# One SBUF port in the order planner, the first loads and clears in another order, and the last two steps of a weight's conversion on VectorE unless late

## The chip, the cores and the metric

The kernel runs on one core of a Trainium2 chip. The metric is the device time of one execution in microseconds (us); of the kernel before, three timed runs are given. The profiled execution is one more run, and its span (first to last instruction) lies inside its own time.

## The reference

Causal attention with a cumulative bias, and two matrix-product blocks behind it. All is float32, and the weights arrive as float64 words that the kernel converts itself.

```
scores = q @ k.T / sqrt(64)                      # 4 batches, 8 heads, 576 tokens, 64 wide
cum    = cumsum(max(s, 0))
scores = where(causal, -1e9, scores + min(-(cum[:, None] - cum[None, :]), 0))
x      = softmax(scores) @ v                     # -> [2304, 512]
x      = (s2 * relu(x @ w_in)**2 + b) @ w_out    # 512 -> 2048 -> 512
out    = max(x @ w1, x @ w2, x @ w3) @ w_fin     # 512 -> 3 x 768 -> 512
```

## The kernel before

A float32 product is made of three passes of a split pair: each operand has a part `hi` and a rest `lo` in the matmul type, and `mm3` (L224) multiplies hi by hi, hi by lo and lo by hi. So every operand has a `lo` step, a subtraction (`minus`, L221/222), behind its `hi` step.

The work stands in four stages. **Attention** goes in jobs of two heads: the first four jobs do the first 320 queries of a batch (part A), the next four the other 256 (part B), the other twelve a whole batch's pair of heads (part W). In a job `turn` transposes q and k (L430), `qk` makes scores (L447) and adds the bias with a one-hot row times the table `dd` (L449), `least` (L461) takes the row minimum on VectorE, `expo` (L467) is on ScalarE, `turn_p` transposes the probabilities (L508), `av` multiplies by v (L527), and `x_copy` (L532) leaves the result. **The first block, part a** uses half of the 2048 columns (`wa_in`, `wa_out`), and its matmuls fill whatever TensorE leaves free beside attention. **Part b** uses the other half (`wb_in`, `wb_out`, converted beside attention and parked in DRAM) in eight halves of a batch. **The second block** (`wt`, `wfin`) ends the run.

A weight piece is converted in nine steps (`weight_steps`, L240): a load, an ACT step (`wsa`/`stage`/`wg`, L255), four VectorE steps (L258, L260, L264, L266), the `hi` copy (L215 on ACT), and the two last ones, step 7 (L222: the rest of `hi`) and step 8 (L270: the sum that is `lo`). 16 pieces of 128x512 belong to part a, 32 of 128x256 to part b, 24 of 128x384 to `wt`, and 6 of 128x512 to `wfin`.

The order on every engine is fixed ahead of the run by `Plan.order` (L81): a list of steps with a cost on one or several engines, a priority and needs. It takes at each point the engine with the earliest start, and there the step of best priority. Where a step names two engines, the first is the rule, and the second is taken when it would be done earlier by more than LATE (L52). So the engine named first matters, and in `convert` (L687) the last two steps name GpSimd (Pool) first:

```
shift, either = dve_fast(n) - 0.06, {"Pool": pool_(n), "DVE": dve(n)}
```

Before the plan's steps come the clears and the bias table in written order (L306 to L358): `s` is loaded four times on 32 partitions each, VectorE sums it up (L316) and makes five differences `df` (L321), ScalarE rounds and VectorE splits them into `dd` (L324). GpSimd clears `qn`, `kn`, `vn` (L342) and the tails of the probability tiles `pp` (L351). SP issues the loads of q, k, v and weights in its own order.

Of the kernel before, what the change touches and what calls it, by code (L numbers as in the profile page):

```python
# [8 lines left out]
F32 = mybir.dt.float32  # L9
# [9 lines left out]
P = 128  # L19
# [4 lines left out]
ST2 = 3  # L24
COLD = 15

# [32 lines left out]
class Plan:  # L59
# [21 lines left out]
    def order(self):  # L81
        n = len(self.steps)
# [57 lines left out]
        for done in range(n):  # L140
# [34 lines left out]
def fused_kernel(ctx, tc, q, k, v, s, w_in, w_out, ms, mb, w1, w2, w3, w_fin, out,  # L175
# [142 lines left out]
    df = atp.tile([P, OFF[-1] + W[-1]], F32, name="df", tag="p2")  # L318
    for i in range(NC):
        mid = QS[i] + QN[i] // 2  # L320
        nc.vector.tensor_scalar(df[:, OFF[i]:OFF[i] + W[i]], cum[:, :W[i]], -1.0, cum[:, mid:mid + 1], op0=ALU.mult, op1=ALU.add)  # L321
    for a, b in ((0, OFF[3]), (OFF[3], OFF[4]), (OFF[4], OFF[4] + W[4])):
        nc.scalar.activation(dh[:, :b - a].bitcast(F32R), df[:, a:b], AF.Copy)
        nc.vector.scalar_tensor_tensor(dd[:, a:b], dh[:, :b - a], lower, df[:, a:b], op0=ALU.mult, op1=ALU.add)  # L324


# [11 lines left out]

    qn, kn = (atp.tile([P, NC, 2, D], F32, name=x) for x in ("qn", "kn"))
    vn = [atp.tile([P, NC, 2, D], F32, name=f"vn{i}") for i in range(2)]  # L340
# [8 lines left out]
    for j in range(2):  # L349
        for i in range(NC):  # L350
            nc.gpsimd.memset(pp[j][i][:, W[i]:], 0.0)  # L351
        nc.gpsimd.memset(pp[j][0][LAST:, :], 0.0)

# [240 lines left out]
    add(("begin",), {"SP": 1.05}, 0, -1e9, [], lambda: None)  # L594
    add(("s_b",), "SP", (2, 2), 30.0, [], load_sb)
    jobs = [Job(n, n % NP, "AB"[n // NP]) if n < 2 * NP else Job(n, n - NP, "W") for n in range((B + 1) * NP)]
    t0 = 0.0
    for job in jobs:
# [26 lines left out]
        for x, u in enumerate(units):  # L625
# [3 lines left out]
            ready = [("oh", n)] + [("copy", z, n, y) for z in "qk" for y in range(2)]  # L629
            add(("qk", n, u), "PE", 5 * (k1 - k0) / 2400 + 0.25, at[u], ready + [("after", z) for z in same] + order, qk, job, u,  # L630
                take=[("sm", [("least", n, u, j)]) for j in range(2)], **a)
# [14 lines left out]
        for x, u in enumerate(units):  # L646
            i, k0, k1, c0, c1 = UNITS[u]
            for j in range(2):
# [3 lines left out]
                m = (c1 - c0) * QN[i]  # L652
                add(("turn_p", n, u, j), "PE", 0.109 * (c1 - c0), t, [("exp", n, i, j)] + order, turn_p, job, u, j, take=[("sm", [("copy_p", n, u, j)])], **a)
                over, take = [("after", ("copy_p", n, units[0], j))], []
# [32 lines left out]
    def convert(name, z, piece, stage_tile, prios, needs, ring_st, ring_a, **k):  # L687
# [3 lines left out]
        def step(on=None):  # L691
# [390 lines left out]
```

## Time and profile before

| what | us |
| --- | --- |
| median of three runs (range) | 1014.78 (1014.14 to 1016.34) |
| the profiled execution, its own time | 1016.21 |
| its span | 1014.4 |
| TensorE (PE) busy in the span | 965.1 |
| VectorE (DVE) busy | 496.7 |
| ScalarE (ACT) busy | 451.2 |
| GpSimd (POOL) busy | 307.4 |

TensorE is busy for 95% of the span. Its busy time counts pipelined matmuls with modelled ends, so a busy stretch need not be one at peak, and the granted clock says whether it ran at 2.4 or 1.2 GHz. What any change can take away is the time in which TensorE is idle or at the lower clock.

### The profile page before, as it was taken

Reading aid. Unit: us, or ns where it says so; the run is one execution under the profiler, and the core shown is the slowest. Engines: PE = TensorE matmul, PEld = TensorE weight load, DVE = VectorE, ACT = ScalarE, POOL = GpSimd, SP = SyncE. Lnnn points to the kernel's source line nnn. Section 1 sums busy time; section 2 is a strip of 40 time slices with the busy share of each in tenths; the row PEclk is TensorE's granted clock in tenths of the full one; section 3 lists DMA queues with packets and bytes.
Section 4 is the critical chain, followed back from the end, with each engine's and each line's share of the span. In section 5 each row is a group of like instructions: output and inputs, shape, how many; then the busy total and the mean of one; then the engine's idle time right before and its main releaser. Section 6 shows DMA issues by size and latency. Waiting matters only on the chain.

```text
span 1014.4 us, 17966 instructions
## 1 busy us (share of the span) xinstructions
PE 965.1 (95%) x6532; PEld 877.1 (86%) x6532; DVE 496.7 (49%) x1205; ACT 451.2 (44%) x1210; POOL 307.4 (30%) x398
## 2 busy tenths in 40 slices
PE   3878899999999999999989899999999999999998
PEld 2656788878789779999979899999999999999997
DVE  5888677776752341222799943323942222222221
ACT  4866787877865573332444443334321212121111
POOL 4564444554422103222576732222510000000000
PEclk9889899999999999999989899999999999999999
DMA  6554256556630300381255451313201010100000
GB/s 169 149 159 120 63 169 188 152 162 177 175 85 23 86 17 26 132 306 54 81 156 162 126 170 54 88 38 106 90 16 47 16 47 17 48 16 32 1 32 32
DMA packets 120633, 96.12 MB, mean 95 GB/s; under 512 B 70240, under 2 KB 104032, under 8 KB 120544
## 3 DMA queue, kind: packets, MB, share of 16 engines
q1 hardware_dynamic: 120448, 94.82, 32.0%
q8 instruction: 52, 0.85, 0.4%
q14 instruction: 37, 0.30, 0.1%
q10 hardware_dynamic: 96, 0.15, 0.0%
HBM read 67.67 MB, written 27.26 MB: 94 GB/s over the span
## 4 chain that ended last, share of the span: by engine, by line
PE 78%; DVE 9%; DMA 4%; issue 4%; POOL 3%; ACT 2%; SPq 0%; POOLq 0%; DVEq 0%; ACTq 0%
PE mm L226 20%; PE mm L227 20%; PE mm L228 20%; PE ps L447 5%; PE pt L508 5%; PE px L527 4%; PE pr L430 2%; PE ps L449 1%; POOL gbl L222 1%; DMA qn<-in_q_dram 1%; DMA xs<-x_d 1%; DVE g L849 1%; DVE wsa L258 1%; PE pr L498 1%; DVE wsa L260 1%
## 5 line engine op out<-in xcount | busy, mean ns | idle before, releaser
L226 PE MATMUL mm<-yh,wt 128*128 128x384 f32 x432 | 146.2, 339 | 0.0
L228 PE MATMUL mm<-yh,wt 128*128 128x384 f32 x432 | 146.2, 338 | 0.0
L227 PE MATMUL mm<-yl,wt 128*128 128x384 f32 x432 | 146.2, 338 | 0.0
L999 DVE TENSOR_TENSOR u<-mm,u 128x384 f32<-128x384 f32 x72 | 40.1, 556 | 186.5 <-PE mm L228 186.4
L853 ACT ACTIVATE g<-g 128x256 f32<-128x256 f32 (+1 forms) x128 | 56.5, 442 | 127.3 <-DVE g L849 127.0
L849 DVE TENSOR_SCALAR g<-mm 128x256 f32<-128x256 f32 (+1 forms) x128 | 58.3, 456 | 96.3 <-PE mm L228 82.0
L467 ACT ACTIVATE pp<-pp,mn 64x64 f32<-64x64 f32 (+4 forms) x160 | 88.4, 555 | 27.4 <-DVE mn L461 27.2
L227 PE MATMUL mm<-gbl,wb_out 128*128 128x320 f32 (+2 forms) x256 | 79.4, 310 | 10.3 <-POOL gbl L222 10.2
L508 PE MATMUL pt<-ident,pp 128*128 128x128 f32 x480 | 80.6, 287 | 6.3 <-DVE mn L461 3.0
L222 POOL TENSOR_TENSOR ga<-g,ga 128x320 fp32r<-128x320 f32 (+1 forms) x60 | 49.0, 817 | 120.3 <-ACT ga L215 106.8
L226 PE MATMUL mm<-xhi,wa_in 128*128 128x320 f32 (+1 forms) x256 | 83.4, 326 | 0.0
L222 POOL TENSOR_TENSOR gbl<-g,gbh 128x256 fp32r<-128x256 f32 (+1 forms) x61 | 52.5, 861 | 100.3 <-ACT gbh L215 100.2
L447 PE MATMUL ps<-k,q 64*128 64x288 f32 (+4 forms) x384 | 75.4, 455 | 7.5 <-DVE mn L461 5.8
L226 PEld LDWEIGHTS mm<-yh,wt 128*128 128x128 f32 x432 | 81.1, 188 | 1.3
L227 PEld LDWEIGHTS mm<-yl,wt 128*128 128x128 f32 x432 | 81.1, 188 | 1.3
L226 PE MATMUL mm<-ga,wa_out 128*128 128x320 f32 (+2 forms) x256 | 82.0, 320 | 0.0
L228 PEld LDWEIGHTS mm<-yh,wt 128*128 128x128 f32 x432 | 81.1, 188 | 0.0
L461 DVE CUSTOM_DVE_ANT_0 pp<-late_keys,ps 64x64 f32<-64x64 f32 (+4 forms) x160 | 61.7, 421 | 38.1 <-PE ps L449 37.9
L215 ACT ACTIVATE pt<-pt 128x256 f32<-128x256 f32 (+3 forms) x184 | 73.4, 432 | 15.3 <-PE pt L508 14.1
L226 PE MATMUL mm<-gbh,wb_out 128*128 128x320 f32 (+2 forms) x256 | 78.0, 305 | 0.8 <-ACT gbh L215 0.6
L227 PE MATMUL mm<-xlo,wa_in 128*128 128x320 f32 (+1 forms) x256 | 76.9, 300 | 0.8 <-POOL xlo L222 0.8
L228 PE MATMUL mm<-gbh,wb_out 128*128 128x320 f32 (+2 forms) x256 | 77.5, 303 | 0.0
(176 smaller groups left out, 2453.6 us busy)
## 6 DMA issues: line engine op xcount, KB each, us to landing
wst<-in_moe_w_dram SPq DMA_DIRECT2D x24, 384.0 KB, 3.4
wb_d<-wbs SPq DMA_DIRECT2D x21, 256.0 KB, 2.9
out_dram<-o SPq DMA_DIRECT2D x18, 256.0 KB, 2.1
kn<-in_k_dram SPq DMA_DIRECT2D x32, 128.0 KB, 3.0
vn<-in_v_dram SPq DMA_DIRECT2D x32, 128.0 KB, 2.7
wst<-in_moe_w_out_dram SPq DMA_DIRECT2D x8, 512.0 KB, 3.9
wb_in<-wb_d SPq DMA_DIRECT2D x8, 512.0 KB, 7.6
wb_out<-wb_d SPq DMA_DIRECT2D x8, 512.0 KB, 9.1
```

The costliest lines, as they stand in the source:

```text
L215: nc.scalar.activation(dst, src, AF.Copy, scale=1.0 if scale is None else scale)
L222: ENGINES[on].tensor_tensor(dst, a, b, op=ALU.subtract)
L226: nc.tensor.matmul(ps, lhs[0], rhs[0], start=first, stop=False)
L227: nc.tensor.matmul(ps, lhs[0], rhs[1], start=False, stop=False)
L228: nc.tensor.matmul(ps, lhs[1], rhs[0], start=False, stop=last)
L447: nc.tensor.matmul(ps[:, :k1 - k0], qt[job.n][r, QS[i]:QS[i] + P], kt[job.n][r, k0:k1], start=True, stop=False)
L461: nc.vector.tensor_tensor_reduce(out=pp[j][i][:n, k0:k1], in0=late_keys[:n, a:a + k1 - k0], in1=ps_.pop((job.n, u, j))[:n, :k1 - k0], scal ...
L467: nc.scalar.activation(p[:n, :w], p[:n, :w], AF.Exp, bias=mns[job.n, j][:n, i:i + 1], scale=-1.0, accum_out=sums[job.n % 2][:n, j, i:i + 1])
L508: nc.tensor.transpose(pt[:, c - c0, :], pp[j][i][:, c * P:(c + 1) * P], ident)
L527: nc.tensor.matmul(px_[job.n][hf][j * D:(j + 1) * D, a0 - h0:h1 - h0], vn[job.n % 2][:, c, j, :], columns(job, pr["p", job.n, j], c, c + 1 ...
L849: nc.vector.tensor_scalar(st["g", f], st["u", f][:, :n], 0.0, None, op0=ALU.max)
L853: nc.scalar.activation(st["g", f], st["g", f], AF.Square)
```

## The change

The planner gets a table of steps that it counts as users of one SBUF port of VectorE and GpSimd together: every GpSimd step, and on VectorE every weight step and the named ones in PORT. Such a step starts in the plan no earlier than the other engine's last such step ends, less 0.1 us. Nothing in the hardware is switched; only the planned order moves. COLD, the time in which the plan doubles TensorE's costs, goes from 15 to 8.

The last two steps of a weight's conversion name VectorE first, and GpSimd only when late. The four loads of `s` go to ScalarE's queue, so SP starts with q and k. `qn` and `kn` are cleared on VectorE and `vn` on GpSimd, and only the partitions of the short chunks. The bias differences 3 and 4, and the tails of `pp` 3 and 4, become planned steps behind a "pre" step for each engine's opening. 26 transposes of the identity open TensorE's row.

```diff
-COLD = 15
+COLD = 8
+WARM = 26
...
+    PORT = ("square", "lo", "hi", "x_hi", "x_lo", "xb_lo", "lo_h", "lo_y")
+    OVERLAP = 0.1
...
+        port = {"Pool": 0.0, "DVE": 0.0}
+
+        def has_port(i, e):
+            key = self.steps[i][0]
+            return e == "Pool" or e == "DVE" and (key[0] == "w" or key[0] in self.PORT or key[0][:-1] in self.PORT)
...
+            if has_port(i, e):
+                t = max(t, port["DVE" if e == "Pool" else "Pool"] - self.OVERLAP)
...
     for g in range(4):
-        (nc.sync if g < 2 else nc.scalar).dma_start(s0[g * NH:(g + 1) * NH], s.rearrange("b h s -> (b h) s"))
+        nc.scalar.dma_start(s0[g * NH:(g + 1) * NH], s.rearrange("b h s -> (b h) s"))
+    SHORT = (SPLIT // P, NC - 1)
+    for t in (qn, kn):
+        for c in SHORT:
+            nc.vector.memset(t[LAST:, c], 0.0)
...
-    for t in (qn, kn, *vn):
-        nc.gpsimd.memset(t[D:, :, :, :], 0.0)
+    for t in vn:
+        for c in SHORT:
+            nc.gpsimd.memset(t[LAST:, c], 0.0)
...
+    def warm():
+        ps = bank("warm")
+        for _ in range(WARM):
+            nc.tensor.transpose(ps[:, :P], ident, ident)
...
+    for e, cost in (("DVE", 8.2), ("ACT", 7.3), ("Pool", 5.0)):
+        add(("pre", e), e, cost, -1e9, [], lambda: None)
+    add(("warm",), "PE", 0.213 * WARM / 2, -1e9, [], warm, take=[("sm", [("warm",)])])
+    for i in range(3, NC):
+        add(("dd", i), "DVE", 2.2, 1.0 + i, [("pre", "DVE")], rest_d, i, att=True)
+    add(("pp",), "Pool", 1.2, 4.0, [("pre", "Pool")], rest_p, att=True)
...
+        either2 = {"DVE": dve(n), "Pool": pool_(n)}
...
-                 ("DVE", shift, (4,), []), ("DVE", dve(n), (5,), []), (either, 0, (6,), []), (either, 0, (7,), []))
+                 ("DVE", shift, (4,), []), ("DVE", dve(n), (5,), []), (either2, 0, (6,), []), (either2, 0, (7,), []))
```

What the order becomes is seen best in three places. The first is SP's row of DMA issues from the start, before (`qn`, `kn`, `vn` are q, k and v tiles, 128x2x64 full chunks and 64x2x64 the short one; `wg` and `stage` hold a 512 KB weight piece):

```order
L309 DMA s_123<-in_s_dram 32x576 x2
L406 DMA qn<-in_q_dram 64x2x64
L406 DMA kn<-in_k_dram 64x2x64
L251 DMA wg<-in_moe_w_in_dram 128x512
L406 DMA vn_159<-in_v_dram 64x2x64
L251 DMA wg<-in_moe_w_in_dram 128x512
L406 DMA vn_160<-in_v_dram 64x2x64
L251 DMA wg<-in_moe_w_in_dram 128x512
L404 DMA qn<-in_q_dram 128x2x64 x2
L404 DMA kn<-in_k_dram 128x2x64 x2
```

The same row with the change:

```order
L429 DMA qn<-in_q_dram 128x2x64 x2
L431 DMA qn<-in_q_dram 64x2x64
L429 DMA kn<-in_k_dram 128x2x64 x2
L431 DMA kn<-in_k_dram 64x2x64
L266 DMA wg<-in_moe_w_in_dram 128x512
L429 DMA vn_130<-in_v_dram 128x2x64 x2
L431 DMA vn_130<-in_v_dram 64x2x64
L266 DMA wg<-in_moe_w_in_dram 128x512
L429 DMA vn_131<-in_v_dram 128x2x64 x2
L431 DMA vn_131<-in_v_dram 64x2x64
L266 DMA wg<-in_moe_w_in_dram 128x512
L266 DMA stage<-in_moe_w_in_dram 128x512 x2
```

The full chunks of the first q and k moved ahead of all weights; five weight pieces, where there were three, now stand ahead of the second job's q, which follows this piece of the row.

The second place is GpSimd's row in the second half of part b, before (`gbl` is the `lo` of an activation that TensorE's next product waits for, `wsa` and `wt` are steps 7 and 8 of a weight piece):

```order
L222 TENSOR_TENSOR wsa<-wsa,wt_6105 128x384
L222 TENSOR_TENSOR gbl_6113<-g,gbh_6112 128x256
L222 TENSOR_TENSOR gbl_6113<-one 128x2
L222 TENSOR_TENSOR gbl_6115<-g,gbh_6114 128x256
L222 TENSOR_TENSOR gbl_6115<-one 128x2
L270 TENSOR_TENSOR wt_6105<-wsa,wst 128x384
L222 TENSOR_TENSOR gbl_6117<-g,gbh_6116 128x256
L222 TENSOR_TENSOR gbl_6117<-one 128x2
L222 TENSOR_TENSOR wsa<-wsa,wt_6105 128x384
```

And with the change:

```order
L237 TENSOR_TENSOR gbl_6142<-g,gbh_6141 128x256
L237 TENSOR_TENSOR gbl_6142<-one 128x2
L237 TENSOR_TENSOR gbl_6144<-g,gbh_6143 128x256
L237 TENSOR_TENSOR gbl_6144<-one 128x2
L237 TENSOR_TENSOR gbl_6146<-g,gbh_6145 128x256
L237 TENSOR_TENSOR gbl_6146<-one 128x2
```

The weight steps have left GpSimd's row; in all of part b it holds nothing but `gbl`.

The third is VectorE's row in the same half, before (`g` is the relu that leaves PSUM):

```order
L258 TENSOR_SCALAR wsa<-wsa 128x384
L849 TENSOR_SCALAR g<-mm 128x256
L260 SCALAR_TENSOR_TENSOR wsa<-wst,wsa 128x384
L849 TENSOR_SCALAR g<-mm 128x256
L264 TENSOR_SCALAR wst<-wsa 128x384
L266 SCALAR_TENSOR_TENSOR wst<-wst 128x384
L258 TENSOR_SCALAR wsa<-wsa 128x384
L849 TENSOR_SCALAR g<-mm 128x256
L260 SCALAR_TENSOR_TENSOR wsa<-wst,wsa 128x384
L849 TENSOR_SCALAR g<-mm 128x256
```

And with the change:

```order
L896 TENSOR_SCALAR g<-mm 128x256
L237 TENSOR_TENSOR wsa<-wsa,wt_6133 128x384
L273 TENSOR_SCALAR wsa<-wsa 128x384
L285 TENSOR_TENSOR wt_6133<-wsa,wst 128x384
L896 TENSOR_SCALAR g<-mm 128x256
L275 SCALAR_TENSOR_TENSOR wsa<-wst,wsa 128x384
L273 TENSOR_SCALAR wsa<-wsa 128x384
L896 TENSOR_SCALAR g<-mm 128x256
L279 TENSOR_SCALAR wst<-wsa 128x384
L275 SCALAR_TENSOR_TENSOR wsa<-wst,wsa 128x384
L896 TENSOR_SCALAR g<-mm 128x256
```

Steps 7 and 8 came in between the relus, mostly two weight steps to a relu as before. Over the whole program all 48 such steps of `wt` and all 12 of `wfin` are on VectorE with the change (3 and 0 before); of part a's 32 it has 25 (7 before), and of part b's 64 it has 60 (4 before). On TensorE 39 groups of three part-a matmuls stand ahead of the eighth job's `av`, where 30 stood.

## Rows read from the trace of the kernel before

**Rows 1.** Stretches: length; PE, PEld, DVE, ACT, POOL busy; PE clock; DMA share; GB/s

```profile
0.00:12.80 12.80, 0.00 (x0) 0.02 (x1) 6.85 (x17) 3.22 (x4) 8.62 (x32) 1.00 0.67 191
12.80:125.00 112.20, 93.36 (x592) 69.80 (x593) 86.42 (x211) 77.23 (x227) 56.34 (x62) 0.88 0.47 125
125.00:482.00 357.00, 355.56 (x2787) 308.33 (x2785) 175.18 (x589) 215.16 (x643) 120.63 (x179) 1.00 0.42 125
482.00:604.90 122.90, 111.73 (x770) 107.45 (x769) 102.86 (x171) 56.66 (x136) 78.45 (x81) 0.93 0.48 139
604.90:707.00 102.10, 102.10 (x771) 102.10 (x770) 31.58 (x64) 35.50 (x80) 25.94 (x32) 1.00 0.26 72
707.00:1014.40 307.40, 302.36 (x1622) 289.36 (x1620) 93.78 (x153) 63.46 (x122) 17.46 (x12) 1.00 0.11 34
```

**Rows 2.** What TensorE waited for up to 125 us (total, times, longest)

```profile
PE pr L430 <- DMA qn<-in_q_dram: 15.3, 2, 12.8
PE ps L447 <- DVE mn L461: 5.8, 3, 2.6
```

**Rows 3.** What TensorE waited for, 482 to 605 us

```profile
PE mm L227 <- POOL gbl L222: 10.2, 11, 1.4
```

**Rows 4.** Timeline of the opening (start, length, engine, idle before)

```profile
0.73 0.89 ACTq L309 DMA_DIRECT2D s<-in_s_dram  x2
...
3.69 0.46 DVE L315 TENSOR_SCALAR s<-s 128x576 f32<-128x576 f32 x1 [1.96 <-DMA s<-in_s_dram]
...
7.43 0.80 DVE L324 SCALAR_TENSOR_TENSOR dd<-s,lower,df 128x576 fp32r<-128x576 f32 x1
...
12.81 0.88 PE L430 MATMUL pr<-ident,qn 128*128 128x128 f32 x3 [12.81 <-DMA qn<-in_q_dram]
...
15.30 0.40 PE L449 MATMUL ps<-dd,oh 64*128 64x64 f32 x2
```

**Rows 5.** TensorE's timeline where jobs 0 and 1 go on

```profile
18.93 0.81 PE L447 MATMUL ps<-k,q 64*128 64x320 f32 x4
...
23.54 0.69 PE L447 MATMUL ps<-k,q 64*128 64x64 f32 x4
```

**Rows 6.** Stretches up to 10 us, columns as in rows 1; GB/s stands last

```profile
0.00:5.00 5.00, 0.00 (x0) 0.00 (x0) 2.04 (x9) 1.28 (x1) 4.10 (x15) 1.00 0.37 88
5.00:10.00 5.00, 0.00 (x0) 0.00 (x0) 4.00 (x8) 1.55 (x3) 4.52 (x18) 1.00 0.86 277
```

**Rows 7.** Issues of q's loads: size each, median us to landing

```profile
qn<-in_q_dram SPq DMA_DIRECT2D x24, 128.0 KB, 3.1
```

**Rows 8.** Part a's tile stage: count, min/median/max ns

```profile
L260 DVE SCALAR_TENSOR_TENSOR stage<-stage x8: 682/1088/1801, 32.7 to 112.2; 128x512 int32<-128x512 int32 x8
...
L222 POOL TENSOR_TENSOR stage<-stage,wa_out x6: 1266/1465/1714, 62.1 to 116.2; 128x512 f32<-128x512 f32 x6
...
L222 DVE TENSOR_TENSOR stage<-stage,wa_out x2: 678/682/687, 91.5 to 111.1; 128x512 f32<-128x512 f32 x2
```

**Rows 9.** The tile wsa, all of its steps: count, min/median/max ns

```profile
L258 DVE TENSOR_SCALAR wsa<-wsa x30: 347/656/1537, 486.5 to 735.8; 128x384 int32<-128x384 int32 x24, 128x512 int32<-128x512 int32 x6
L260 DVE SCALAR_TENSOR_TENSOR wsa<-wst,wsa x30: 544/1036/1681, 487.3 to 737.4; 128x384 int32<-128x384 int32 x24, 128x512 int32<-128x512 int32 x6
L264 DVE TENSOR_SCALAR wst<-wsa x30: 343/364/973, 489.6 to 738.1; 128x384 int32<-128x384 int32 x24, 128x512 int32<-128x512 int32 x6
...
L222 POOL TENSOR_TENSOR wsa<-wsa,wt x23: 999/1227/1329, 491.6 to 589.0; 128x384 f32<-128x384 f32 x23
...
L270 DVE TENSOR_TENSOR wt<-wsa,wst x2: 546/688/831, 493.7 to 501.9; 128x384 fp32r<-128x384 f32 x2
```

**Rows 10.** TensorE's timeline where the first, fifth half of part b and the second block begin

```profile
482.02 0.30 PE L226 MATMUL mm<-xbh,wb_in 128*128 128x320 f32 x1
...
604.92 0.31 PE L226 MATMUL mm<-xbh,wb_in 128*128 128x320 f32 x1
...
707.00 0.34 PE L226 MATMUL mm<-yh,wt 128*128 128x384 f32 x1
```

More of the change, by code (lines that the diff above doesn't have):

```diff
@@ L154, in order @@
             free[e] = end[i]
+            if has_port(i, e):
+                port[e] = end[i]
             for o in costs:
@@ L308, in fused_kernel @@
     for g in range(4):
-        (nc.sync if g < 2 else nc.scalar).dma_start(s0[g * NH:(g + 1) * NH], s.rearrange("b h s -> (b h) s"))
+        nc.scalar.dma_start(s0[g * NH:(g + 1) * NH], s.rearrange("b h s -> (b h) s"))
+    qn, kn = (atp.tile([P, NC, 2, D], F32, name=x) for x in ("qn", "kn"))
+    vn = [atp.tile([P, NC, 2, D], F32, name=f"vn{i}") for i in range(2)]
+    SHORT = (SPLIT // P, NC - 1)
+    for t in (qn, kn):
+        for c in SHORT:
+            nc.vector.memset(t[LAST:, c], 0.0)
     nc.vector.memset(ones, 1.0)
@@ L318, in fused_kernel, with difference, split_d @@
     df = atp.tile([P, OFF[-1] + W[-1]], F32, name="df", tag="p2")
-    for i in range(NC):
+    def difference(i):
         mid = QS[i] + QN[i] // 2
         nc.vector.tensor_scalar(df[:, OFF[i]:OFF[i] + W[i]], cum[:, :W[i]], -1.0, cum[:, mid:mid + 1], op0=ALU.mult, op1=ALU.add)
-    for a, b in ((0, OFF[3]), (OFF[3], OFF[4]), (OFF[4], OFF[4] + W[4])):
+    def split_d(a, b):
         nc.scalar.activation(dh[:, :b - a].bitcast(F32R), df[:, a:b], AF.Copy)
         nc.vector.scalar_tensor_tensor(dd[:, a:b], dh[:, :b - a], lower, df[:, a:b], op0=ALU.mult, op1=ALU.add)
+    for i in range(3):
+        difference(i)
+    split_d(0, OFF[3])
     groups = ident.rearrange("p (a g t) -> p a g t", a=4, t=2)
@@ L337, in fused_kernel @@
     nc.gpsimd.affine_select(out=late_keys[:, ZK - P:], in_=late_keys[:, ZK - P:], pattern=[[-1, P]], compare_op=ALU.is_ge, fill=BIG, base=0, channel_multiplier=1)
-    qn, kn = (atp.tile([P, NC, 2, D], F32, name=x) for x in ("qn", "kn"))
-    vn = [atp.tile([P, NC, 2, D], F32, name=f"vn{i}") for i in range(2)]
-    for t in (qn, kn, *vn):
-        nc.gpsimd.memset(t[D:, :, :, :], 0.0)
+    for t in vn:
+        for c in SHORT:
+            nc.gpsimd.memset(t[LAST:, c], 0.0)
     sums = [atp.tile([P, 2, NC], F32, name=f"sums{z}") for z in range(2)]
@@ L349, in fused_kernel @@
     for j in range(2):
-        for i in range(NC):
+        nc.gpsimd.memset(pp[j][0], 0.0)
+        for i in range(1, NC - 2):
             nc.gpsimd.memset(pp[j][i][:, W[i]:], 0.0)
-        nc.gpsimd.memset(pp[j][0][LAST:, :], 0.0)
     pick = atp.tile([P, NC, P], F32R, name="pick")
@@ L415, in load_v, with rest_d, rest_p @@
         load_tokens(vn[job.n % 2], v, job.p, 0, job.keys)
+    def warm():
+        ps = bank("warm")
+        for _ in range(WARM):
+            nc.tensor.transpose(ps[:, :P], ident, ident)
+    def rest_d(i):
+        difference(i)
+        split_d(OFF[i], OFF[i] + W[i])
+    def rest_p():
+        for j in range(2):
+            for i in range(NC - 2, NC):
+                nc.gpsimd.memset(pp[j][i][:, W[i]:], 0.0)
     def one_hot(job):
@@ L629, in fused_kernel @@
             ready = [("oh", n)] + [("copy", z, n, y) for z in "qk" for y in range(2)]
-            add(("qk", n, u), "PE", 5 * (k1 - k0) / 2400 + 0.25, at[u], ready + [("after", z) for z in same] + order, qk, job, u,
+            add(("qk", n, u), "PE", 5 * (k1 - k0) / 2400 + 0.25, at[u], ready + [("dd", i) if i > 2 else ("pre", "DVE")] + [("after", z) for z in same] + order, qk, job, u,
                 take=[("sm", [("least", n, u, j)]) for j in range(2)], **a)
@@ L652, in fused_kernel @@
                 m = (c1 - c0) * QN[i]
-                add(("turn_p", n, u, j), "PE", 0.109 * (c1 - c0), t, [("exp", n, i, j)] + order, turn_p, job, u, j, take=[("sm", [("copy_p", n, u, j)])], **a)
+                add(("turn_p", n, u, j), "PE", 0.109 * (c1 - c0), t, [("exp", n, i, j), ("pp",) if i > 2 else ("pre", "Pool")] + order, turn_p, job, u, j, take=[("sm", [("copy_p", n, u, j)])], **a)
                 over, take = [("after", ("copy_p", n, units[0], j))], []
```

## The prediction

> **What bounds the kernel now.** I read the stretches first [rows 1], to see where TensorE loses time, since nothing else can be won. It is idle for 12.8 us at the start. From 12.8 to 125 us it is busy for 93.36 of 112.2 us, and the mean granted clock is 0.88: between the two levels, full (2.4 GHz) and half (1.2 GHz), that is half clock for 24% of the time, some 27 us. From 125 to 482 us it has 1.4 us of idle time and full clock, so nothing is to be had there. From 482 to 604.9 us it is busy for 111.73 of 122.9 us at 0.93. After that it is full up to 707 us, and idle for 5 us in the rest.
>
> Then I read what TensorE waited for. In the opening it is the load of q, 15.3 us in two waits, and behind it VectorE's row minimum, 5.8 us in three [rows 2]. From 482 to 605 us it is one thing: GpSimd's `gbl`, 10.2 us in 11 waits [rows 3].
>
> The size of that second loss comes from TensorE's timeline [rows 10]. Part b is eight halves of the same work in pairs. The first four take from 482.02 to 604.92, 122.9 us; the last four from there to 707.00, 102.1 us with TensorE full. So 20.8 us are lost in the first four: 11.2 us idle, and the rest to the half clock that follows the gaps.
>
> What differs between the fours is the conversion of `wt`. GpSimd is busy for 78.45 us in the first and 25.94 in the second, VectorE for 102.86 and 31.58 [rows 1]. And the two disturb each other: the same VectorE step takes 347 ns at its shortest and 1537 at its longest, another 544 and 1681 [rows 9], while steps 7 and 8 of the conversion hold GpSimd for 1.0 to 1.3 us each. The `gbl` that TensorE needs stands in line behind them.
>
> **The change in part b (482 to 605 us).** 45 steps of `wt` leave GpSimd, which then has `gbl` alone, as in the last four halves: 26 us of work in 123 [rows 1]. That wait goes. What is late next is VectorE. Its work for a piece is four steps now and six then. At their shortest the four are 0.35, 0.54, 0.34 and 0.55 (the fourth as the second, its nearest row), and the two new ones 0.55 each [rows 9]: 2.88 us, for 24 pieces 69 us. The rest of its work is what it does in the last four halves, 31.6 us [rows 1]. Together 101 us, against 102.1 us that TensorE needs. So VectorE is just enough if its steps run at their shortest, and the conversion itself has time: `wt` is first needed at 707 us [rows 10], and in the new row the pieces are done within the first four halves. What cannot wait are the relus, which stand behind one or two weight steps each, as they did.
>
> Bounds for this part: all of the loss goes, 20.8 us; or VectorE becomes the bound and none does. I take 15 us, nearer the first, because the conversion steps now meet GpSimd's 0.8 us `gbl` at most once per relu instead of also 1.0 to 1.3 us weight steps.
>
> The Trainium skill, SBUF — State Buffer, section Who interferes with whom, says that a VectorE instruction with two SBUF inputs contends with a GpSimd instruction that reads SBUF, and that one then blocks the other for a whole instruction. The trace agrees in kind: 544 ns alone, up to 1681 beside GpSimd [rows 9]. Under that rule the moved steps are still not free, since each still meets `gbl`; with 69 us of weight steps, 16 `xbl` at 0.54 and 26 us of `gbl` in one line it gives 104 us as the least for the four halves, a gain of 19 instead of 20.8 us, and no slack.
>
> **The opening (0 to 20 us).** q and k go ahead of the weights. Their loads land some 3.1 us after issue [rows 7], so near 4 to 6 us instead of 12.8 [rows 4]. But then the bias table is late next. All four loads of `s` now leave from ScalarE's row, which took 0.89 us for two [rows 4], so 1.8 for four; and the fourth waits for the semaphore of an earlier load, by the row's waits. With a landing of 2.1 us (from 1.6 to 3.69) `s` is there at 4.6 us if that wait costs nothing, and near 6.3 us if it waits for q; I take the second. From the landing of `s` to the end of the first piece of `dd` it is 4.5 us (3.69 to 8.23, [rows 4]), so the first bias product comes at about 10.8 us instead of 15.30: 4.5 us early. The 26 transposes take 7.6 us at the pace of three in 0.88 us [rows 4], from the making of the identity on, and so end before that; without this cover q's own transposes would wait for them, 3 us or so.
>
> Then the next q is late. Five weight pieces stand ahead of it, where three stood ahead of the first. Ahead of the second q there are now `s` 0.29, q and k 0.33, v 0.33 and weights 2.62, 3.6 MB. With 0.44 MB moved by 5 us (88 GB/s) and 277 GB/s after [rows 6] that is near 16.4 us. In the new row of TensorE the last unit of job 0 stands behind the second q's transposes, so it comes at about 17 instead of 18.93 [rows 5], and job 1, behind the third q, issued then and landing 3.1 us later, at about 20.5 instead of 23.54. I take 3 us for the opening, with bounds of 1 and 5.
>
> **The rest up to 125 us.** By the orders, 15 of steps 7 and 8 move from GpSimd to VectorE ahead of the eighth job's result: 15 x 0.68 = 10 us on VectorE, and 15 x 1.46 = 22 of 56 us off GpSimd [rows 1, 8]. Three casts and copies go from VectorE to ScalarE, 2 us at that price. Against that stand shorter waits: a two-input step has a median of 1088 ns and a minimum of 682 here [rows 8], and each of the 16 pieces has two. If those 0.4 x 32 = 13 us fall with GpSimd's busy time, by 22 of 56, VectorE saves 5 us. 10 - 2 - 5: its load stays within 3 us of what it is, 86 of 112 us [rows 1]. So I expect no gain from VectorE's load. A gain comes from TensorE's gaps: nine groups more of part-a matmuls stand ahead of that job, 27 matmuls at a pace of 0.13 us (102.1 us for 771 records, [rows 1]), 3.5 us that now run in gaps. Bounds: the rest of the 18.8 us of idle time and of the half clock, and VectorE's 10 - 2 us without the 5, less what its 26 us of idle time covers; that is +12 and -6. I take +3.5.
>
> **Elsewhere.** From 125 to 482 us 56 steps of part b's weights move to VectorE. It is idle for 182 of 357 us [rows 1], which covers them: at half the width and so half of 0.68 us [rows 8] they are 19 us, which TensorE would wait for without this cover. The 12 of `wfin` fall after 707 us, where VectorE is busy for 94 of 307 us [rows 1]. I put both at nothing, with 3 us of loss as the other end. Clears and the tails of `pp` are done long before the job that reads them.
>
> **The sum.** 15 + 3 + 3.5 = 21.5 us. The profiled execution took 1016.2 us for a span of 1014.4, and 1016.2 - 21.5 = 994.7. It lies 1.4 us above the median of the runs, so the median should come out at 993.3, and I say 993.
>
> **The rivals.**
> - VectorE becomes the bound in part b. For it: 101 us of work in 102.1 us. Against it: the conversion can be late without harm, and the relus stand where they stood. Then part b gains nothing and the time is 1014.8 - 6.5 = 1008.
> - The opening gives back what it gains: the row minimum that TensorE waits for [rows 2] stands behind more weight steps on VectorE, and no wait on GpSimd's weight steps is in that list. Then only part b gains: 1014.8 - 15 = 1000.
> - Slower: the steps moved to VectorE are stretched as much as their neighbours. In the first four halves VectorE is busy for 102.86 us, of which 31.6 belongs to other work, so a piece costs 2.97 us for four steps; two more at 0.74 make 4.45 us, 107 us for all, with the rest 138.4 us instead of 122.9, and relus late by that much: 1014.8 + 15.5 - 6.5 = 1024. It decides from 4.1 us a piece on: (122.9 + 6.5 - 31.6) / 24. Against it: what stretches them, GpSimd's weight steps, is gone.
> - The change does nothing that counts: both gains are eaten within 2 us: 1014.
>
> **How the numbers follow.** Forecast (985 to 999) 0.60; VectorE the bound 0.13; only part b 0.13; slower 0.07; nothing 0.07. Below 978 both parts would have to give nearly their upper bounds. The range 977 to 1008 leaves out the slower case, the unchanged one and half of the VectorE case. Two us, 0.2%, is about what a measurement of this kernel can tell from no change. Faster 0.86, within 0.2% 0.07, slower 0.07.
>
> **What would show it.** TensorE's first bias product near 11 us, and job 1's scores near 20. From part b's first matmul to its fifth half 102 to 112 us instead of 122.9, GpSimd near 26 us busy there, the wait of `mm` for `gbl` gone from the list, and VectorE's L260 near 0.55 us. The time up to 482 us down by about 7. I am wrong if TensorE waits there for `g` or for its banks instead, if the granted clock stays at 0.93 in part b, or if the row minimum's waits before 125 us grow by more than the opening saves.

## The result and the profile after

| kernel | median of its runs, us (range) | ratio to before, 95% interval |
| --- | --- | --- |
| before | 1015.56 (1014.14 to 1016.8) | |
| after | 977.9 (977.39 to 979.69) | 0.9633 [0.9613, 0.9652] |

The change gives 37.7 us; the forecast was a gain of 21.5, a time of 993. The measured 977.9 lies outside the 985 to 999 that had a chance of 0.60, and 0.9 us above the low end of the range, 977. The profiled execution of after has a span of 976.5 us, 37.9 less than before.

The stretches of after come first, with the columns of [rows 1] and the cuts at the same places of the program.

```profile
0.00:12.80 12.80, 6.28 (x44) 5.83 (x44) 7.32 (x29) 4.60 (x10) 5.52 (x30) 0.96 0.70 187
12.80:125.00 112.20, 101.01 (x711) 76.75 (x712) 90.25 (x261) 86.84 (x257) 37.78 (x49) 0.91 0.57 150
125.00:462.00 337.00, 336.12 (x2649) 291.24 (x2650) 172.44 (x588) 206.09 (x620) 76.68 (x124) 1.00 0.41 125
462.00:567.00 105.00, 103.37 (x771) 102.53 (x770) 97.63 (x211) 57.92 (x136) 31.18 (x40) 1.00 0.53 154
567.00:669.10 102.10, 102.10 (x771) 102.10 (x770) 31.77 (x65) 35.50 (x80) 25.96 (x32) 1.00 0.28 80
669.10:976.50 307.40, 302.33 (x1622) 289.31 (x1620) 90.16 (x165) 64.22 (x122) 0.00 (x0) 1.00 0.11 34
```

The last two stretches are as long as before, 102.1 and 307.4 us. Part b's first four halves take 105.0 us where they took 122.9 [rows 1]. Everything else was gained ahead of part b, which starts at these places of TensorE's timeline:

```profile
461.99 0.30 PE L241 MATMUL mm<-xbh,wb_in 128*128 128x320 f32 x1
...
566.99 0.31 PE L241 MATMUL mm<-xbh,wb_in 128*128 128x320 f32 x1
...
669.06 0.34 PE L241 MATMUL mm<-yh,wt 128*128 128x384 f32 x1
```

Against [rows 10] that is 482.02 - 461.99 = 20.0 us by the start of part b and 122.9 - 105.0 = 17.9 us in it, together the 37.9 of the span. The forecast had 6.5 and 15.

From 125 us to part b TensorE is full in both kernels; what differs there is how much work is left, 2649 records where 2787 were [rows 1]. So nearly all of the 20 us was gained by 125 us. The stretch from 36 to 125 us shows how, first of before, then of after:

```profile
36.00:125.00 89.00, 73.99 (x480) 55.72 (x481) 70.78 (x166) 59.71 (x172) 47.74 (x54) 0.88 0.44 116
```

```profile
36.00:125.00 89.00, 84.90 (x633) 65.92 (x633) 79.87 (x229) 73.88 (x213) 35.88 (x45) 1.00 0.59 151
```

Busy time by granted clock makes 73.99 x 0.88 = 65.1 us at the full clock of 2.4 GHz before and 84.9 after: 19.8 us, about the gain. Before, TensorE idled for 15 us there, and after gaps of 0.6 to 2.6 us the clock stood at half for some of the time. After, it idles for 4.1 us and the clock stays full. VectorE does more work there, GpSimd less.

In part b the wait for `gbl`, 10.2 us in 11 waits [rows 3], is nearly gone. TensorE's waits from 462 to 567 us:

```profile
PE mm L242 <- POOL gbl L237: 1.6, 4, 0.6
```

And the tile `wsa` shows VectorE's steps at their shortest, as against [rows 9]; the last two rows are the moved steps:

```profile
L273 DVE TENSOR_SCALAR wsa<-wsa x30: 344/356/701, 466.5 to 694.0; 128x384 int32<-128x384 int32 x24, 128x512 int32<-128x512 int32 x6
L275 DVE SCALAR_TENSOR_TENSOR wsa<-wst,wsa x30: 541/552/1096, 467.2 to 694.9; 128x384 int32<-128x384 int32 x24, 128x512 int32<-128x512 int32 x6
L279 DVE TENSOR_SCALAR wst<-wsa x30: 345/354/891, 468.4 to 696.1; 128x384 int32<-128x384 int32 x24, 128x512 int32<-128x512 int32 x6
L237 DVE TENSOR_TENSOR wsa<-wsa,wt x24: 545/552/1256, 471.0 to 565.7; 128x384 f32<-128x384 f32 x24
L285 DVE TENSOR_TENSOR wt<-wsa,wst x24: 541/554/1234, 472.6 to 566.3; 128x384 fp32r<-128x384 f32 x24
```

The median of L275 (L260 before) fell from 1036 to 552 ns. That is why VectorE, with 45 weight steps more there, is busy for 97.63 us and not more than the 102.86 of before.

The opening of after, in its timeline:

```profile
1.74 4.55 PE L446 MATMUL warm<-ident 128*128 128x128 f32 x26 [1.74 <-POOL ident masks.py:199]
...
5.52 0.46 DVE L336 TENSOR_SCALAR s<-s 128x576 f32<-128x576 f32 x1 [3.06 <-DMA s<-in_s_dram]
...
9.90 0.30 PE L489 MATMUL ps<-dd,oh 64*128 64x64 f32 x2
...
19.22 0.88 PE L470 MATMUL pr<-ident,qn 128*128 128x128 f32 x3 [8.53 <-DMA qn<-in_q_dram]
...
20.03 1.44 PE L487 MATMUL ps<-k,q 64*128 64x320 f32 x4
...
25.30 0.69 PE L487 MATMUL ps<-k,q 64*128 64x64 f32 x4
```

The first bias product is 5.4 us earlier than in [rows 4], but then TensorE waits 8.53 us for the second q. Job 0's last unit is 1.1 us and job 1's first unit 1.8 us later than in [rows 5].

### The profile page after: what moved, and what is told of

It reads as the page before. It is cut to its first block, busy times and chain, and to the rows that moved or that the text cites. A ratio compares the mean times of both kernels' runs of the same rounds, so it can differ in the third digit from the quotient of the medians.

```text
span 976.5 us, 17902 instructions
## 1 busy us (share of the span) xinstructions
PE 951.2 (97%) x6558; PEld 867.8 (89%) x6558; DVE 489.6 (50%) x1317; ACT 455.2 (47%) x1223; POOL 177.1 (18%) x275
## 4 chain that ended last, share of the span: by engine, by line
PE 82%; DVE 7%; DMA 4%; ACT 3%; issue 2%; SPq 1%; POOL 1%; DVEq 0%; ACTq 0%; POOLq 0%
PE mm L241 21%; PE mm L243 20%; PE mm L242 20%; PE ps L487 6%; PE pt L548 6%; PE px L567 5%; PE pr L470 2%; PE ps L489 1%; DVE wsa L237 1%; DMA wst<-in_moe_w_dram 1%; DVE wt L285 1%; DMA xs<-x_d 1%; DVE g L896 1%; PE pr L538 1%; DVE wst L281 1%
## 5 line engine op out<-in xcount | busy, mean ns | idle before, releaser
L507 ACT ACTIVATE pp<-pp,mn 64x64 f32<-64x64 f32 (+4 forms) x160 | 88.5, 557 | 21.1 <-DVE mn L501 20.9
L241 PE MATMUL mm<-ga,wa_out 128*128 128x320 f32 (+2 forms) x256 | 82.4, 322 | 0.1
L230 ACT ACTIVATE pt<-pt 128x384 f32<-128x384 f32 (+3 forms) x187 | 75.0, 436 | 15.0 <-PE pt L548 14.0
L237 POOL TENSOR_TENSOR gbl<-g,gbh 128x320 fp32r<-128x320 f32 (+1 forms) x64 | 53.5, 836 | 150.1 <-ACT gbh L230 150.1
L1050 ACT ACTIVATE hh<-u 128x384 fp32r<-128x384 f32 x36 | 18.9, 525 | 131.6 <-DVE u L1046 131.6
L548 PE MATMUL pt<-ident,pp 128*128 128x128 f32 x480 | 77.7, 282 | 1.6 <-ACT rb L230 0.7
L242 PE MATMUL mm<-gbl,wb_out 128*128 128x320 f32 (+2 forms) x256 | 75.9, 297 | 1.6 <-POOL gbl L237 1.6
L237 POOL TENSOR_TENSOR ga<-g,ga 128x320 fp32r<-128x320 f32 (+1 forms) x64 | 53.3, 834 | 131.8 <-ACT ga L230 116.2
L242 PE MATMUL mm<-ga,wa_out 128*128 128x320 f32 (+2 forms) x256 | 76.0, 297 | 0.8 <-POOL ga L237 0.8
L243 PE MATMUL mm<-ga,wa_out 128*128 128x320 f32 (+2 forms) x256 | 75.9, 296 | 0.6 <-DVE wa_out L285 0.6
L243 PE MATMUL mm<-xbh,wb_in 128*128 128x320 f32 (+1 forms) x256 | 75.8, 296 | 0.0
```

The lines of the kernel that those rows point to most:

```text
L230: nc.scalar.activation(dst, src, AF.Copy, scale=1.0 if scale is None else scale)
L237: ENGINES[on].tensor_tensor(dst, a, b, op=ALU.subtract)
L241: nc.tensor.matmul(ps, lhs[0], rhs[0], start=first, stop=False)
L242: nc.tensor.matmul(ps, lhs[0], rhs[1], start=False, stop=False)
L243: nc.tensor.matmul(ps, lhs[1], rhs[0], start=False, stop=last)
L507: nc.scalar.activation(p[:n, :w], p[:n, :w], AF.Exp, bias=mns[job.n, j][:n, i:i + 1], scale=-1.0, accum_out=sums[job.n % 2][:n, j, i:i + 1])
```

## The experiments

All in one table: the time, the ratio to before, and from each profiled execution where part b starts and how long its first four halves take. The labels are those of the sections below. Each ratio is to the kernel before as it ran beside that kernel (medians from 1014.84 to 1016.44), so where two rows of the table are compared, a difference of 1 us in the medians says little.

| kernel | median us | ratio, 95% interval | part b starts | four halves |
| --- | --- | --- | --- | --- |
| before | 1015.56 | | 482.02 | 122.90 |
| after | 977.9 | 0.9633 [0.9613, 0.9652] | 461.99 | 105.00 |
| move alone | 980.75 | 0.9663 [0.9645, 0.9682] | 460.97 | 109.36 |
| port rule alone | 1000.18 | 0.9857 [0.9821, 0.9893] | 479.86 | 109.16 |
| opening alone | 1015.71 | 1.0006 [0.9997, 1.0015] | 480.01 | 123.39 |
| move and port rule | 978.13 | 0.9635 [0.9617, 0.9652] | 461.96 | 105.95 |
| after without the move | 994.71 | 0.9796 [0.9777, 0.9816] | 475.24 | 107.13 |
| after, idle GpSimd additions | 1014.82 | 0.9996 [0.9983, 1.0009] | 475.19 | 127.15 |
| after, small GpSimd additions | 995.01 | 0.9791 [0.9777, 0.9804] | 466.84 | 118.42 |
| after, SP in the plan's order | 982.95 | 0.9683 [0.9664, 0.9702] | 464.80 | 106.33 |
| after, one transpose | 978.6 | 0.9632 [0.9606, 0.9659] | 459.39 | 107.82 |
| move, port rule, SP in the plan's order | 982.72 | 0.9679 [0.9659, 0.9699] | 466.91 | 105.94 |
| after, second q on ScalarE's queue | 978.47 | 0.9629 [0.9615, 0.9642] | 461.77 | 105.76 |
| the same, one transpose | 977.43 | 0.9624 [0.961, 0.9637] | 459.23 | 105.92 |

### Which part gives it

**The move alone**, in the kernel before:

```diff
-                 ("DVE", shift, (4,), []), ("DVE", dve(n), (5,), []), (either, 0, (6,), []), (either, 0, (7,), []))
+                 ("DVE", shift, (4,), []), ("DVE", dve(n), (5,), []), (either2, 0, (6,), []), (either2, 0, (7,), []))
```

with `either2 = {"DVE": dve(n), "Pool": pool_(n)}`.

> The kernel before with one edit: steps 7 and 8 of every weight's conversion name VectorE first. Theory M (the moved steps gave both gains): the first product on xbh starts at 462 to 466 (482.02 before, 461.99 after), the four halves behind it take 105 (122.9 before), the whole 978 to 986. Theory P (the planner's port rule gave the 20 us ahead of 482) and theory O (the new opening did): the product starts at 480 to 484, the four halves take 105, the whole is 995 to 1000.

Measured 980.75, part b from 460.97, theory M, though the four halves take 109.36 us where it had 105. The opening is that of before, and still part b starts 21.1 us earlier.

**The port rule alone** (`has_port`, `port`, `PORT` and `OVERLAP` of the change, nothing else):

> The kernel before with the planner's port rule and nothing else; GpSimd keeps steps 7 and 8. Theory M: no gain in either stage, first product on xbh at 478 to 484, four halves 120 to 124, the whole 1008 to 1017. Theory P: first product at 462 to 466, the halves 120 to 124, the whole 993 to 998. Theory O: as theory M.

Measured 1000.18: none of the three. It gains 2.2 us ahead of part b, as theories M and O have it, and 13.7 us in it, which none had. Its stretch of the four halves and TensorE's wait there:

```profile
479.90:589.00 109.10, 104.59 (x769) 102.66 (x769) 87.74 (x155) 55.62 (x132) 78.28 (x81) 1.00 0.48 136
```

```profile
PE mm L240 <- POOL gbl L235: 3.3, 5, 1.2
```

GpSimd is as busy as before (78.28 us against 78.45), yet `gbl` is late by a third. Fewer conversion steps fall into the stretch: GpSimd has 41 of `wt` there where it had 45, and VectorE 155 instructions in all where it had 171. How the rule comes to that order was not taken further.

Ahead of part b this kernel is of use for the cause. Its waits for the row minimum `mn` up to 125 us are down to 1.5 us, from 9.5 before, and yet TensorE's full-clock work from 36 to 125 us rises only from 65.1 to 74.55 x 0.93 = 69.3 us:

```profile
36.00:125.00 89.00, 74.55 (x507) 55.45 (x507) 68.92 (x164) 61.72 (x170) 55.84 (x59) 0.93 0.48 125
```

```profile
PE pt L521 <- DVE mn L474: 1.2, 1, 1.2
...
PE pr L443 <- DVE mn L474: 0.3, 1, 0.3
```

TensorE now stops for part a's weights `wa_out`, whose steps 7 and 8 GpSimd still does, 7.0 us in three waits:

```profile
117.53 0.41 PE L241 MATMUL mm<-ga,wa_out 128*128 128x320 f32 x1 [0.86 <-POOL wa_out L283]
120.70 0.64 PE L239 MATMUL mm<-ga,wa_out 128*128 128x320 f32 x1 [2.76 <-ACT wa_out L228]
125.02 0.64 PE L241 MATMUL mm<-ga,wa_out 128*128 128x320 f32 x1 [3.42 <-POOL wa_out L283]
```

So fewer waits for `mn` alone do not give the 20 us.

**The opening alone**: the kernel after with

```diff
-            return e == "Pool" or e == "DVE" and (key[0] == "w" or key[0] in self.PORT or key[0][:-1] in self.PORT)
+            return False
```

and `either` in place of `either2`.

> The kernel after without the port rule and with steps 7 and 8 back on GpSimd first, so only the opening (loads, clears, planned differences and tails, 26 transposes) is new. Theory M: first product on xbh at 479 to 486, since job 1's last unit was 1.8 us later in the opening of after than of before, four halves 123, the whole 1012 to 1019. Theory O: first product at 462 to 466, the whole 994 to 999. Theory P: as theory M.

Measured 1015.71, theory M: the interval of the ratio holds 1. Part b starts 2.0 us earlier, but the time does not show it.

**The move and the port rule**, in the kernel before:

> The kernel before with steps 7 and 8 on VectorE and the port rule, the opening of before. Theory M: the same as the move alone within 3 us, 975 to 986. Theory P: 975 to 981, some 18 below the move alone. Theory O: 995 to 1000, some 20 above the kernel after.

Measured 978.13, as the kernel after, theory M. It is 2.6 us below the move alone; the intervals overlap, so the port rule's share behind the move is not settled by the times. In the trace the four halves are 3.4 us shorter.

**The kernel after without the move** (`either` in place of `either2`):

> The kernel after with one edit undone: steps 7 and 8 name GpSimd first again. If the parts add up (port rule alone 14.8 us, opening alone nothing): first product on xbh at 478 to 482, four halves 107 to 111, the whole 997 to 1003, so the move is worth some 22 us in the kernel after. If the opening gives something once the plan is honest on GpSimd: 985 to 995. If the port rule needs the old opening: 1005 or more.

Measured 994.71, at the edge of the second case, so my sum failed: 5.5 us better than the port rule alone, though the opening alone is worth nothing. With the port rule and without the move the opening does give something; with both it gives nothing (977.9 against 978.13). The parts do not add up. The move is worth 16.8 us on top of the other two and 34.3 us by itself.

### Why the move gives it

**Idle GpSimd additions.** The kernel after, with the moved steps on VectorE, and work of the same size on GpSimd that no product waits for:

```diff
+    def extra(on, low):
+        if on == "DVE":
+            low = low.rearrange("p (a n) -> p a n", n=P)
+            same = ident.unsqueeze(1).to_broadcast(low.shape)
+            nc.gpsimd.tensor_tensor(low, same, same, op=ALU.add)
...
         on = yield
+        extra(on, word(F32, 0))
         minus(a, a, hi.bitcast(F32), on)
         on = yield
+        extra(on, word(F32, 0))
```

> The kernel after, and beside each moved step an addition on GpSimd of the same 512 or 256 elements (identity plus identity, into the staging tile's dead low words) that no product waits for; the output is unchanged. Theory L (GpSimd's elementwise work by itself slows VectorE, wherever its result goes): VectorE's stretch over the shortest of each form from 12.8 to 125 us goes from 12 to 20 or more, TensorE waits 5 to 10 us for mn again, first product on xbh at 470 to 484, four halves 110 to 123, the whole 988 to 1016. Theory C (the weight itself was late, since its last two steps were slow; nobody minds GpSimd's load): first product on xbh at 461 to 465, four halves 105 to 108, the whole 977 to 983.

Measured 1014.82: the whole gain is gone, theory L, with the four halves (127.15 us) above its range. That the time is just that of before is chance: part b still starts 6.8 us earlier than before, its four halves take 4.2 us longer, and what follows them 2 us longer. The order on every engine is that of after, but for the additions. Stretches, then `wsa`, then TensorE's wait in part b:

```profile
36.00:125.00 89.00, 78.73 (x540) 58.85 (x542) 85.04 (x191) 65.76 (x187) 59.82 (x64) 0.96 0.48 126
...
475.20:602.30 127.10, 114.56 (x770) 109.57 (x769) 120.58 (x211) 57.50 (x136) 79.82 (x87) 0.92 0.44 126
```

```profile
L237 DVE TENSOR_TENSOR wsa<-wsa,wt x24: 543/998/1182, 484.2 to 601.1; 128x384 f32<-128x384 f32 x24
L293 DVE TENSOR_TENSOR wt<-wsa,wst x24: 543/831/1187, 485.7 to 601.6; 128x384 fp32r<-128x384 f32 x24
```

```profile
PE mm L242 <- POOL gbl L237: 10.9, 12, 1.7
```

VectorE does the same 211 instructions as after in 120.58 us instead of 97.63. The medians of the moved steps rise from 552 and 554 to 998 and 831 ns, and the minima stay. So GpSimd's work slows VectorE even where no product waits for its result. The SBUF — State Buffer page of the Trainium skill, section Who interferes with whom, has a VectorE instruction with two SBUF inputs contend with a GpSimd instruction that reads SBUF; by that rule the trace agrees. But I had expected TensorE to wait 5 to 10 us for `mn` up to 125 us, and it waits 1.9: what is late there is spread over several tiles.

**Small GpSimd additions.** GpSimd taken for about as long, with at most a twelfth of the data:

```diff
-            low = low.rearrange("p (a n) -> p a n", n=P)
-            same = ident.unsqueeze(1).to_broadcast(low.shape)
-            nc.gpsimd.tensor_tensor(low, same, same, op=ALU.add)
+            for i in range(low.shape[1] // 96):
+                nc.gpsimd.tensor_tensor(low[:, 8 * i:8 * i + 8], ident[:, :8], ident[:, :8], op=ALU.add)
```

> As the kernel with idle GpSimd additions, but in place of each addition of 512 (384, 256) elements a row five (four, two) additions of 8 elements a row, which by the durations of small additions on GpSimd (0.20 to 0.24 us) keep it about as long, with at most a twelfth of the data. The output is unchanged. Theory E (the price is the data that GpSimd moves while VectorE works): VectorE's instructions stay as short as in the kernel after, four halves 105 to 109, the whole 977 to 985. Theory T (the price is the time for which GpSimd is taken, so that its own bias halves and sums come late): first product on xbh at 470 to 478, four halves 118 to 128, the whole 1000 to 1016.

Measured 995.01, between the theories, so both prices are real. Again stretches, `wsa`, and the wait:

```profile
36.00:125.00 89.00, 80.04 (x593) 62.31 (x594) 80.79 (x215) 71.77 (x205) 66.32 (x161) 1.00 0.53 139
...
466.80:585.30 118.50, 108.69 (x771) 106.55 (x770) 99.12 (x212) 57.76 (x136) 84.57 (x231) 0.96 0.47 137
```

```profile
L237 DVE TENSOR_TENSOR wsa<-wsa,wt x24: 543/550/1093, 475.9 to 583.6; 128x384 f32<-128x384 f32 x24
L292 DVE TENSOR_TENSOR wt<-wsa,wst x24: 543/550/1233, 476.8 to 584.1; 128x384 fp32r<-128x384 f32 x24
```

```profile
PE mm L242 <- POOL gbl L237: 9.7, 8, 1.8
```

VectorE is as fast as in after (550 ns; 99.12 us busy), and GpSimd is busy for 84.57 us in part b, even a little more than with the large additions, part of it time in which an addition stands behind a VectorE step (last section). What is left is GpSimd's queue: `gbl` stands behind the additions, and TensorE waits 9.7 us for it. So of the 36.9 us that the large additions cost, GpSimd's being taken accounts for 17.1 (995.01 - 977.9; 16 by the ratios) and the slowed VectorE, as the difference, for the other 19.8 (21 by the ratios). By the table's two last columns the first price is 4.9 us ahead of part b and 13.4 in it, the second 8.4 and 8.7; another 2.0 of the second fall behind part b's four halves. One more thing goes with the first price: an addition also holds the staging tile, and up to 125 us the weight loads on SP wait 10.9 us for the small ones. What that makes of the 4.9 us was not separated; in part b TensorE's only listed wait is for `gbl`.

### Why the opening gives nothing

**SP in the plan's order.** In all kernels above, SP's row of DMA issues is not the plan's:

```diff
-MANUAL = lambda nc: {x.engine for x in (nc.tensor, nc.scalar, nc.vector, nc.gpsimd)}
+MANUAL = lambda nc: {x.engine for x in (nc.tensor, nc.scalar, nc.vector, nc.gpsimd, nc.sync)}
```

> The kernel after, with SP's row put in the plan's order too, so the second q and k are issued behind two weight pieces instead of five; the rows of the other engines stay as they are. Theory Q (the 8.53 us in which TensorE waits for the second q, and the half clock up to 32 us, are lost for good): the second q lands at 12 to 14 instead of 19.22, job 1's last unit ends near 20 instead of 25.30, and the whole is 4 to 8 us shorter, 970 to 974. Theory Q0 (what is lost there is filled later, or VectorE sets the pace up to 125 us): 976 to 979. A third: SP now waits in the plan's order and keeps weights or stores behind it, 980 to 990.

Measured 982.95, 5 us worse, the third case. The second q's transposes start at 12.57 us instead of 19.22 and the first job's result comes 8.4 us earlier. It is given back, as I read it, in these steps of the timeline (`x` is a job's result, `x_d` its store):

```profile
27.77 0.48 DVE L572 TENSOR_TENSOR x<-px,rb 128x320 f32<-128x320 f32 x1
...
32.05 0.38 SPq L584 DMA_DIRECT2D x_d<-x  x1
...
36.88 0.49 DVE L572 TENSOR_TENSOR x<-px,rb 128x320 f32<-128x320 f32 x1 [3.33 <-DMA x_d<-x]
...
38.76 0.19 DVE L515 RECIPROCAL rs<-rs 128x6 f32<-128x6 f32 x1
...
40.09 0.47 PE L526 MATMUL pr<-ident,rr 128*128 128x128 f32 x1 [3.07 <-POOL rr L522]
```

The store of the first `x` leaves SP 4 us after it is made, behind loads. The second `x` needs that buffer, so VectorE stands still for 3.33 us, the sums behind it are late, and TensorE waits 3.07 us for `rr`. Then the clock is at half for a while. From 36 to 51 us, here and in after:

```profile
36.00:51.00 15.00, 11.85 (x61) 8.07 (x60) 11.80 (x30) 9.63 (x31) 5.71 (x7) 0.66 0.46 119
```

```profile
36.00:51.00 15.00, 12.85 (x103) 9.12 (x102) 14.55 (x46) 14.50 (x50) 5.33 (x8) 1.00 0.70 167
```

**One transpose** in place of 26 (`WARM = 1`):

> The kernel after with one transpose of the identity in place of 26. Theory W (they raise the clock and that is kept): the first scores run at half the clock, the time is 1.5 to 4 us longer, 979.5 to 982. Theory W0 (the clock falls again in the 8.53 us wait for the second q, so they give nothing): 976.5 to 979, no difference.

Measured 978.6, theory W0 by the time. It is not a clean test: SP's own order changed too, and issued the second q at 8.34 us instead of 10.86. Job 1 came earlier, and the store of `x` stopped VectorE for 3.3 us as above.

**The move, the port rule and SP in the plan's order**, in the kernel before:

> The kernel before with the move, the port rule and SP in the plan's order, and the opening of before. Theory Q: the 15.2 us for which TensorE waits on q loads shrink to 6 to 10 and the whole is 972 to 976 (978.13 with SP's own order). Theory Q0: 977 to 980.

Measured 982.72, slower than either theory: also here the shorter wait for q gains nothing, and part b starts 5 us later. The profiled execution took 986.83, more than the median, so its places in the table are late by some of that.

**The second q and k on ScalarE's queue**, which leaves SP's weights where they were:

```diff
-        load_tokens(qn, q, job.p, job.q0, job.q1)
+        load_tokens(qn, q, job.p, job.q0, job.q1, nc.scalar if job.n in (1,) else nc.sync)
...
-        load_tokens(kn, k, job.p, 0, job.keys)
+        load_tokens(kn, k, job.p, 0, job.keys, nc.scalar if job.n in (1,) else nc.sync)
```

(`load_tokens` takes the engine as a further argument.)

> The kernel after, with the second q and k loads issued from ScalarE's queue instead of SP's, so they neither stand behind five weight pieces nor push them back. Theory Q' (the early jobs lose time only if q or the weights are late, and here neither is): the second q lands at 11 to 14, the clock is not at half for longer than some 8 us in all up to 125, the first product on xbh starts at 455 to 459, the whole is 970 to 974. Theory Q0 (an earlier start is given back, as with SP in the plan's order): 976 to 980. Worse than 981 if the two issues hold ScalarE's own copies back.

Measured 978.47, theory Q0, and the second q is still transposed only at 18.77 us. ScalarE's copies of the first q and k now stand behind the issue of the second q, which it reaches at 10.52 us, and the first scores come at 14.21 us instead of 9.61.

**The same with one transpose:**

> The same with one transpose of the identity instead of 26. If the transposes keep the clock up where the long q wait is gone, this one is 1 to 4 us slower than the kernel with them; if they do nothing, the two agree within 1 us, at 970 to 974 or at 976 to 980 by the theories of that kernel.

Measured 977.43, within 1 us of the kernel after; the intervals of the three overlap. So no version that I ran beats the kernel after by more than can be measured, and the 26 transposes show no effect on the time.

## Why the prediction was right in kind and short in size

**Part b, -15: right in mechanism, 2.9 us short.** The wait for `gbl` went from 10.2 to 1.6 us, GpSimd is busy for 31.18 us (26 expected), VectorE's L275 has the expected 0.55 us, VectorE's busy time is 97.63 us of 105.0 (101 of 102.1 expected), and the clock is 1.00. Not slack in VectorE but the fear that it would not keep up made me take 15 instead of 20.8. What I did not price is the port rule: alone it gives 13.7 us here, the move alone 13.5, both 17.0. Either cures most of one wait, so they do not add up. Both causes that I named, the queue ahead of `gbl` and the slowed VectorE, are shown by the two kernels with additions. The other estimate, 104 us as the least for the four halves, comes near the 105.0, but the time does not test it: TensorE alone needs 102.1 there and waits 1.6 for `gbl`.

**The opening, -3: wrong, 0.** The steps up to the first bias product came out (9.90 us, 10.8 expected). The step that failed is "so it comes at about 17 instead of 18.93": the second q was ready at 19.22, not 16.4, and both jobs came later than before, not earlier. The sum took 277 GB/s for all that is moved from 5 us on; in after it is 211 GB/s from 5 to 10 us, 316 from 10 to 15 and 139 from 15 to 20. The 26 transposes were sized wrong too, 4.55 us and not 7.6: three in 0.88 us counts the last one to its end, while in the row they start 0.21 us apart, and 0.11 from 4.8 us on. Yet this is not where the size lies, since the kernels that brought the second q forward by 6 us gained nothing.

**The rest up to 125 us, -3.5: the mis-sized term.** It measured 20, beyond its bound of 12. That bound does not follow from the terms it names: 18.8 us of idle time and 93.36 x 0.12 = 11 us of half clock make 30. The move alone gives the 20: 36 to 125 us goes from 65.1 us of full-clock work to 85.28 in it.

```profile
36.00:125.00 89.00, 85.28 (x638) 65.74 (x640) 83.24 (x236) 72.62 (x215) 29.97 (x43) 1.00 0.60 155
```

The sentence that failed is "So I expect no gain from VectorE's load." The load itself was forecast well, within 3 us of 86 from 12.8 to 125 us, and is 90.25. But what TensorE waits for is not a mean load; it is single steps that come late. Two kinds of them became shorter. GpSimd's halves made single VectorE steps last up to 1.8 us [rows 8]; with those gone the waits for `mn`, 9.5 us in all up to 125 us (5.8 in [rows 2], and the first two rows here), shrink to 0.7 (the third, of after):

```profile
PE pt L508 <- DVE mn L461: 2.7, 2, 1.9
...
PE pr L498 <- DVE mn L461: 1.0, 1, 1.0
```

```profile
PE ps L487 <- DVE mn L501: 0.7, 1, 0.7
```

And part a's own weights come earlier, since a moved step takes 0.68 us where GpSimd took 1.46 [rows 8]: TensorE's first product with `wa_out` stands at 93.8 us in after and at 127.6 before, so there is more to fill its gaps with. With the gaps go the stretches of half clock. That this is the chain is argued, and how the 20 us divide between the two is open: the port rule alone cured most waits for `mn` and was stopped by `wa_out`, and the idle additions cost 13.2 us ahead of part b with 1.9 us of waits for `mn`. What is shown is that the move gives the 20 us, and that work on GpSimd takes 13.2 of them back, with the order on every engine unchanged. I had the row of the 5.8 us [rows 2] and the mean clock of 0.88 [rows 1], and put 3.5 us of new work into the gaps instead of asking what would close them. So that the time still came into the range is luck in part: "below 978 both parts would have to give nearly their upper bounds" did not hold, since the opening gave nothing, part b 17.9 of 20.8, and this term more than its bound. The gaps and the half clock alone were 15 + 73.99 x 0.12 = 24 us from 36 to 125; after they are 4.1.

**Elsewhere, 0: right.** 102.1 and 307.4 us stayed to a tenth.

**The rivals.** "The steps moved to VectorE are stretched as much as their neighbours" has its kernel now, the one with idle additions: there the moved steps do cost 998 and 831 ns and part b takes 127.15 us. It did not come true because GpSimd's own work went away with the move, which was the argument against it. VectorE did not become the bound either: it is busy for 97.63 of the 105.0 us. Of the rival with part b alone one half came true, since the opening gave nothing; its reason did not, as the waits for the row minimum fell, and 20 us were gained ahead of part b.

## What to carry to other kernels

When a step leaves an engine that slows a neighbour, price what the neighbour's short steps in the critical loop gain, by the spread between their shortest and their median, and add the clock that the gaps cost; the mean load of the neighbour says little. Then ask what is late next, as the weights were in the kernel with the port rule alone. An experiment with work that nobody waits for tells the two prices of a busy engine apart: large operands for the slowing, small ones for the queue. A start that is brought forward counts only if the stores and buffers behind it are brought forward as well.

## What the runs showed of the hardware that was not expected

- An addition of 8 elements a row on GpSimd took 198 ns in the median and 192 at the shortest, but 332 in the mean, for some took up to 1774; one of 384 elements took 821 at the shortest and 998 in the mean. So 48 times the data cost four to five times the time.

```profile
L258 POOL TENSOR_TENSOR wst<-ident x272: 192/198/1774, 68.5 to 720.4; 128x8 f32<-128x8 f32 x136
```

- The long ones show that the slowing goes both ways. Of all 497 small additions in the kernel with small GpSimd additions 177 took 300 ns or more, and 145 of these end 53 to 66 ns after the end of a two-input VectorE step (TENSOR_TENSOR or SCALAR_TENSOR_TENSOR): there GpSimd stood until VectorE's step was over.
- The granted clock of the profile does not show a cold start. With one transpose ahead of them, q's three transposes take 0.87 us at 4.03; behind the 26 they take 0.49. The first row is of the kernel with one transpose, the second of after:

```profile
4.03 0.87 PE L470 MATMUL pr<-ident,qn 128*128 128x128 f32 x3 [1.82 <-DMA qn<-in_q_dram]
```

```profile
6.12 0.49 PE L470 MATMUL pr<-ident,qn 128*128 128x128 f32 x3
```

In the first kernel the granted clock reads 1.00 from 0 to 36 us, while at 18.40 us three such transposes still take 0.90 us, as long as in after at 24.47 us, where it reads 0.50. The trace's first entry of the granted clock is a rise, at 24.0 us in the first kernel and at 4.8 in after; before it the row reads 1.00. So up to that entry durations say which level it is, not the row. In the kernel before, the first entry stands at 18.7 us, and three transposes at 12.81 take 0.88 us [rows 4]. So the 0.88 of [rows 1], and the 27 us of half clock that the prediction reads from it, leave out some 6 us.
